# Query loads with four tokens on a partition, one key transposition moved to the DMA queue, one early matmul group moved to another step

## The chip, the core and the metric

The kernel runs on one core of one Trainium2 chip. The core has a matrix engine (TensorE, in the profile PE for its matmuls and PEld for its weight loads), a vector engine (VectorE, DVE), a scalar engine (ScalarE, ACT), a general engine (GpSimd, POOL), and SyncE (SP), which in this kernel only issues DMA transfers. Sixteen DMA engines move the data; all transfers but three of the last stores are issued by SP, one after the other, on one queue. The metric is the device time of one execution in microseconds (us), lower is better.

## The reference, cut to what matters

The first half is a recurrence over 768 tokens, for 4 batches and 8 heads of 64 columns. The second half multiplies its output by four weight matrices.

```
state = zeros(B, H, D, D)                      # B=4, H=8, S=768, D=64
for t in range(S):
    state = gamma[h] * state + outer(k[:, :, t], v[:, :, t])
    y[:, :, t] = scale * q[:, :, t] @ state
x = y.transpose(0, 2, 1, 3).reshape(B * S, H * D)        # 3072 x 512
a = x @ w1;  b = x @ w2                                  # 512 -> 1024
out = ((a * b) @ w3) @ w_out                             # 1024 -> 1024 -> 512
```

Inputs and output are 32-bit floats. Nothing nonlinear stands between w3 and w_out, so the kernel multiplies these two once, at its start.

## The kernel before, in words

**Steps.** The recurrence is worked in chunks of 128 tokens. There are 12 steps, numbered from 0 in the code: steps 0 and 1 (class `Pairs`) take 256 tokens of one batch each, steps 2 to 11 take one chunk of 128 tokens of two batches at a time. The change's title counts from one: its "steps 3 to 12" are 2 to 11 in the code, its "seventh step" is step 6, its "ninth step" is step 8. Below, the code's numbers are used, and kT(6) is the transposed keys of step 6.

**The work of one step.** All of it is in blocks of 64 tokens and 64 columns, four of which lie in the four quarters of the TensorE array at once; those are the "quarters" of the title. `scores(m)` multiplies transposed keys by queries (32 matmuls of 64x64, line 383), VectorE puts the causal mask on the result (line 390), `intra(m)` multiplies the masked scores by the values (32 matmuls, line 531), `kv(m)` forms the new part of the state (32 matmuls, line 551), `inter(m)` multiplies the old state by the queries and adds to the same PSUM banks as `intra` (line 599), and `outputs_back` multiplies by the decay and writes the block of x in half precision (line 614). The feed-forward part follows for the block of an earlier step: 16 groups of 4 matmuls with w1 and w2 (`ab`, line 636), and 16 matmuls with the product of w3 and w_out (`o_unit`, line 663).

**Order.** The order of every engine is written out by hand in `step(m)`; no scheduler moves anything. One pass of `step(m)` on TensorE is: `intra(m-1)`, `kv(m)`, `scores(m)`, `inter(m-1)`, 16 matmuls of `o_unit` for step m-2, 64 matmuls of `ab` for step m-1. Two lists change this. If m is in `EARLY`, `intra(m-1)` already stands in `step(m-1)`, after the second `ab` (four TensorE groups, 16 matmuls). If m is in `K_PE`, the keys of step m+1 are transposed by TensorE in `step(m)` (8 matmuls against an identity, line 357, and a copy by VectorE, line 358); otherwise a DMA transposes them from SBUF to SBUF (`k_dma`, line 363). Where `intra` is not early, `ended` puts a tiny copy on ScalarE behind it, and the first matmul of `inter` waits for that copy[...].

```
    EARLY = (6, 11, 12)
    K_PE = (3, 5)
```

**Queries.** They come in 512 KB tiles, two for every two steps. Tile n = 2g+e holds all 8 heads of one batch e for 256 tokens; a partition holds two consecutive tokens of each head, so that one contiguous piece in memory has 2 x 64 x 4 = 512 bytes. GpSimd casts the tile to half precision and sorts it by token (`q_cast`, line 290), a DMA transposes it (`q_dma`, line 340; the tiles of steps 2 and 3 are transposed by TensorE), and `queries(m, e, p, s, r)` cuts a matmul's moving operand out of it: 64 partitions x 2 runs of 32 columns. The order of the columns, even tokens ahead of odd ones, comes back in the masks `keep` and `keep_t`, in the decays `YS`, and in `outputs_back`, which sorts the tokens into their natural order while it writes (a step of 2 elements).

**The queue.** In `step(m)` SP issues, in this order: kT(m+1) if it is a DMA; the two stores of `o_unit`; one tile of queries for a later step (tile m+3, ahead of the keys and values in even steps, behind them in odd ones); keys and values of step m+2, each as two transfers of 256 KB in pieces of 256 bytes; and in even steps the two transpositions of queries. The loads land in staging buffers (`WST`, 22 of them). SP works strictly in order: a transposition waits on SP for its cast.

Of the kernel before, what the change touches and what calls it, by code (L numbers as in the profile page):

```python
# [12 lines left out]
MULT = mybir.AluOpType.mult  # L13
# [5 lines left out]
def kernel(  # L19
# [11 lines left out]
    nc = tc.nc  # L31
    B, H, S, D = q.shape
    C = 128
    L = 64
    WST = 22
    NCH = S // C
# [4 lines left out]
    TB = 256  # L41
    K_PE = 4

# [15 lines left out]
    def half(x):  # L59
        return slice(x * L, (x + 1) * L)  # L60

    def dma_in(dst, src):
        nc.sync.dma_start(dst, src)  # L63
# [5 lines left out]
    q_in, k_in, v_in = {}, {}, {}  # L69

    def load_q(n):

        g, e = divmod(n, 2)
        if g >= NSTEP // 2:
            return
        bp, cp = divmod(g, NCH // 2)
        q_in[n] = load_pairs(q, bp * 2 + e, cp)

    def load_pairs(src, b, cp):
        t = new_stage()  # L80
        dma_in(
            t[:, :].rearrange("p (h x) -> p h x", x=2 * D),
            src[b, :, cp * 2 * C : (cp + 1) * 2 * C, :].rearrange("h (p t) d -> p h (t d)", t=2),
        )
        return t
# [19 lines left out]
    def new_stage():  # L105
        return wstage.tile([128, 1024], FP, tag="wst", name="stg")
# [18 lines left out]
    for f in range(4, 8):  # L125
        w3_st.append(load_rows(moe_w3, f))
    for e in range(2):
        load_q(e)
        k_in[e] = load_pairs(k, e, 0)
        v_in[e] = load_pairs(v, e, 0)  # L130
    w1_st = [load_rows(moe_w1, d) for d in range(4)]
    w2_st = [load_rows(moe_w2, d) for d in range(4)]
    load_q(2)
    load_q(3)
    for m in range(2, 5):
        load_k(m)
# [14 lines left out]
    for s in range(2):  # L151
        nc.gpsimd.iota(ip_i[half(s), 0:2, :], pattern=[[1, 2], [0, H]], base=1, channel_multiplier=2)
    if_i = const.tile([128, 2, L], mybir.dt.int32, name="if_i")
    nc.gpsimd.iota(if_i[:, :, :], pattern=[[L, 2], [1, 2], [2, 32]], base=1, channel_multiplier=0)
    LGH = const.tile([128, H], FP, name="LGH")
    LGP = const.tile([128, 2, NP], FP, name="LGP")
    for h in range(H):
# [2 lines left out]
    YS = const.tile([128, 3, NP, L], FP, name="YS")  # L160
# [12 lines left out]
    def masks_and_decays():  # L173

        nc.gpsimd.memset(keep[:, :], 1.0)
        for s in range(2):
            r = slice(s * L, (s + 1) * L)
            nc.gpsimd.affine_select(
                out=keep[r, :], in_=keep[r, :], compare_op=mybir.AluOpType.is_ge, fill=0.0,
                base=0, pattern=[[1, 2], [2, 32]], channel_multiplier=-1,  # L180
            )

        nc.gpsimd.memset(keep_t[:, :, :], 1.0)
        for s in range(2):
            for t in range(2):
                nc.gpsimd.affine_select(
                    out=keep_t[half(s), t, :], in_=keep_t[half(s), t, :], compare_op=mybir.AluOpType.is_ge,
                    fill=0.0, base=-t, pattern=[[1, 2], [2, 64]], channel_multiplier=-2,
                )
        for h in range(H):  # L190
            for s in range(2):
                nc.gpsimd.memset(LGP[half((h + s) % 2), s, h // 2 : h // 2 + 1], math.log(gam[h]))
        for h in range(H):
            p, r = h // 2, (h % 2) * 64
            nc.gpsimd.memset(GS[r : r + 64, p : p + 1], gam[h] ** C)
# [11 lines left out]
    XT = {}  # L207
# [70 lines left out]
    q16s, k16s, v16s, qTs, kTs, AMs, psYs, Ts = {}, {}, {}, {}, {}, {}, {}, {}  # L278

    def q_cast(n, *engs):  # L280
        if n not in q_in:
            return
        q16s[n] = att.tile([128, 1024], HP, tag="q16", name="q16", bufs=2)
        pairs_cast(q16s[n], q_in.pop(n), *engs)

    def pairs_cast(dst, src, *engs):
        n = H // len(engs)
        for i, eng in enumerate(engs):
            hs = slice(i * n, i * n + n)
            (nc.scalar.copy if eng is nc.scalar else eng.tensor_copy)(  # L290
                dst[:, :].rearrange("i (t h d) -> i h t d", t=2, d=D)[:, hs, :, :],
                src[:, :].rearrange("i (h t d) -> i h t d", t=2, d=D)[:, hs, :, :],
            )

    def k_cast(m, engs):
        k16 = att.tile([128, 2, 512], HP, tag="k16", name="k16", bufs=3)
        k32 = k_in.pop(m)
        if len(engs) == 1:
            parts = [(k16[:, :, :].rearrange("p e x -> p (e x)"), k32[:, :, :].rearrange("p e x -> p (e x)"))]
        else:  # L300
            parts = [(k16[:, e, :], k32[:, e, :]) for e in range(2)]
        for eng, (dst, src) in zip(engs, parts):
            (nc.scalar.copy if eng is nc.scalar else eng.tensor_copy)(dst, src)  # L303
        k16s[m] = k16
# [57 lines left out]
    def k_dma(m):  # L362
        nc.sync.dma_start_transpose(
            new_kT(m)[:, :, :, :].rearrange("p e a j -> p (e a) j"),
            k16s[m][:, :, :].rearrange("p e x -> p (e x)"),
        )

    def queries(m, e, p, s, r):
        c = m % NCH
        i0 = c % 2 * 64 + s * 32  # L370
        return qTs[m // 2 * 2 + e][half(r), :, p, i0 : i0 + 32]

# [22 lines left out]
    class Pairs:  # L397
# [4 lines left out]

        def k_cast(self, *engs):
            self.k16 = att.tile([128, 1024], HP, tag="k16", name="k16", bufs=3)
            pairs_cast(self.k16, k_in.pop(self.e), *engs)

        def k_transposes(self, tag, on_dve, parts=1):
            self.kT = att.tile([128, 2, NP, 128], HP, tag="kT", name="kT", bufs=2)
# [9 lines left out]
            )  # L418

        def queries(self, r, p, s):  # L420
            return qTs[self.e][half(r), :, p, half(s)]

        def scores(self, t):
            am = att.tile([128, 2, NP, 128], HP, tag="am", name="am")
# [18 lines left out]
        def intra(self, t):  # L443
            if t == 0:
                self.y = [bank(f"Y{s}", [128, NP, 128], FP, "psY") for s in range(2)]
            for p in range(NP):
                for s in range(2):
                    for r in range(2):
                        c0 = p * 128 + r * 64
                        last = nc.tensor.matmul(  # L450
                            self.y[s][half(r), p, :], lhsT=self.v16[half(s), t, c0 : c0 + 64],
                            rhs=self.am[t][half(s), r, p, :], start=(t == 0 and p == 0),
                            stop=(s == 0 and t == 1 and p == NP - 1),
                        )
            return last
# [50 lines left out]
        def outputs_back(self, s):  # L506
            if self.e not in XT:
                XT[self.e] = xpool.tile([128, NP * 2, 2, L], HP, tag="xt", name="xt")
            nc.vector.tensor_tensor(
                XT[self.e][:, :, :, :].rearrange("p (a s) b x -> p a s (b x)", s=2)[:, :, s, :]  # L510
                .rearrange("p a (b i t) -> p a t b i", b=2, t=2),
                self.y[s][:, :, :].rearrange("p a (t b i) -> p a t b i", t=2, b=2),
                YS[:, 0:2, :, :].rearrange("p b a (t i) -> p a t b i", t=2), MULT,
            )


# [68 lines left out]
    def ended(mm, eng=None):  # L585

        mark = (eng.tensor_copy if eng else nc.scalar.copy)(mark_t[:, :], Z[0:1, 0:1])
        wait_for(mark, mm)
        return mark
# [17 lines left out]
    def outputs_back(m, s):  # L607
        if m not in XT:
            XT[m] = xpool.tile([128, NP * 2, 2, L], HP, tag="xt", name="xt")
        swap = s == 1 and m % NCH > 0  # L610
        for to in (half(0), half(1)) if swap else (slice(0, 128),):
            fr = half(1 - to.start // L) if swap else to
            n = fr.stop - fr.start
            nc.vector.tensor_tensor(  # L614
                XT[m][to, :, s, :].rearrange("p (a e) (i t) -> p a e t i", e=2, t=2),
                psYs[m][s][fr, :, :].rearrange("p (a e) (t i) -> p a e t i", e=2, t=2),
                YS[fr, s + swap, :, :].unsqueeze(2).broadcast_to((n, NP, 2, L))
                .rearrange("p a e (t i) -> p a e t i", t=2),
                MULT,
            )  # L620

# [219 lines left out]
    q_cast(3, nc.gpsimd)  # L841
    q_transposes(2, "X0", False)
    k_cast(2, (nc.gpsimd, nc.scalar))
    v_cast(2, (nc.gpsimd, nc.gpsimd))
    for f in range(2):
# [27 lines left out]

    EARLY = (6, 11, 12)

    K_PE = (3, 5)

    def step(m):  # L880

        kv_backs = []
        if m > 4:
            last = None if m in EARLY else ended(intra(m - 1))
            if m < NSTEP:
# [3 lines left out]
        else:  # L889
            inter(m - 1)  # L890
            if m == 4:
                kv_backs.append(kv(m, True))
            am_back = scores(m)
        outputs_back(m - 1, 0)
        outputs_back(m - 1, 1)
        if m >= NSTEP:
            return
        if m + 1 < NSTEP:
            k_cast(m + 1, (nc.gpsimd, nc.gpsimd))
            if m not in K_PE:  # L900
                k_dma(m + 1)
# [11 lines left out]
        for f in range(2):  # L913
            ffn[m - 1].ab(f)
        if m + 1 in EARLY:
            intra(m)
# [15 lines left out]
        for f in range(4, 8):  # L932
            if f == 6 and m in K_PE:
                k_transposes(m + 1, None)
# [43 lines left out]
```

## Time and profile before

| | |
|---|---|
| median of 3 runs | 183.44 us (183.2 to 184.47) |
| span of the profiled execution | 181.5 us |
| TensorE matmuls busy | 175.3 us (97%) |
| VectorE, ScalarE, GpSimd busy | 108.6, 71.9, 71.3 us |
| queue of SP, share of 16 DMA engines | 88.6% |
| q loads (12 of 512 KB), median from issue to landing | 6.4 us |
| k loads (20 of 256 KB), median from issue to landing | 5.6 us |
| transpositions by DMA | 8 of q (4.9 us to landing), 6 of k (4.6 us) |
| transpositions of k by TensorE in line 357 | 32 matmuls, 2.4 us |

How to read it: the busy time of an engine is the union of its instructions, and the span runs from the first instruction to the last. "To landing" is from SP's issue to the semaphore that tells of the last byte, so it contains the time in which the transfer stands in line behind earlier ones. The chain of work that ended last is a list of pieces in order of time, each with start, length and the instructions in it; a piece of "issue" is time in which an engine waited for nothing that the profile shows. In that chain a step is easily found: a block of 3.56 us in line 663 opens the large matmuls of each step, and a block of lines 531, 551, 383 and 599 (`intra`, `kv`, `scores`, `inter`) closes it.

### The profile page before, as it was taken

Reading aid. Unit: us, or ns where it says so; the run is one execution under the profiler, and the core shown is the slowest. Engines: PE = TensorE matmul, PEld = TensorE weight load, DVE = VectorE, ACT = ScalarE, POOL = GpSimd, SP = SyncE. Lnnn points to the kernel's source line nnn. Section 1 sums busy time; section 2 is a strip of 40 time slices with the busy share of each in tenths; the row PEclk is TensorE's granted clock in tenths of the full one; section 3 lists DMA queues with packets and bytes.
Section 4 is the critical chain, followed back from the end, with each engine's and each line's share of the span. In section 5 each row is a group of like instructions: output and inputs, shape, how many; then the busy total and the mean of one; then the engine's idle time right before and its main releaser. Section 6 shows DMA issues by size and latency. Waiting matters only on the chain.

```text
span 181.5 us, 6220 instructions
## 1 busy us (share of the span) xinstructions
PE 175.3 (97%) x2634; PEld 125.4 (69%) x2634; DVE 108.6 (60%) x204; ACT 71.9 (40%) x156; POOL 71.3 (39%) x127
## 2 busy tenths in 40 slices
PE   7889999999999999999999999999999999999992
PEld 2445656688766785876967858768688587685871
DVE  1246658751769669558477584494674956745430
ACT  3354845555631341524334424244243332442431
POOL 3127536964537752725427273055460350000000
PEclk9999999999999999999999999999999999999999
DMA  5999999999999999999999999999999940201203
GB/s 204 376 417 401 298 291 350 409 371 242 194 256 226 182 301 211 203 312 198 245 202 198 295 169 244 190 208 265 236 114 261 178 149 4 116 0 42 78 0 116
DMA packets 79531, 39.71 MB, mean 219 GB/s; under 512 B 57361, under 2 KB 74001, under 8 KB 79505
## 3 DMA queue, kind: packets, MB, share of 16 engines
q1 hardware_dynamic: 79072, 38.81, 88.6%
q8 instruction: 20, 0.33, 0.8%
q10 hardware_dynamic: 432, 0.52, 0.8%
q14 instruction: 7, 0.05, 0.1%
HBM read 29.36 MB, written 6.29 MB: 196 GB/s over the span
## 4 chain that ended last, share of the span: by engine, by line
PE 88%; DMA 5%; ACT 2%; SPq 1%; DVE 1%; issue 0%; ACTq 0%
PE psF L636 41%; PE psO L663 23%; DMA stg<-in_moe_w_out_dram 5%; PE psF L795 4%; PE psW L269 3%; PE psW L255 3%; PE psY L531 2%; PE psY L599 2%; PE psA L383 2%; PE psG L636 2%; PE psK L551 2%; PE psTq L328 1%; PE psW L244 1%; SPq L63 1%; PE psTk L357 1%; PE psY L450 1%
## 5 line engine op out<-in xcount | busy, mean ns | idle before, releaser
L636 PE MATMUL psF<-xt,w 128*128 128x256 f16 x672 | 76.7, 273 | 0.0
L636 PEld LDWEIGHTS <-w 128*128 128x128 f16 x704 | 68.4, 98 | 10.3
L651 DVE TENSOR_TENSOR ht<-pa,psF 128x256 f16<-128x256 f32 x88 | 36.9, 420 | 37.6 <-PE psF L636 32.0
L645 ACT COPY pa<-psF 128x256 f32<-128x256 f32 x80 | 29.8, 373 | 37.5 <-PE psF L636 37.5
L663 PE MATMUL psO<-w3o,ht 128*128 128x512 f16 (+2 forms) x200 | 43.9, 371 | 0.0
L667 ACT ACTIVATE osb<-psO 128x512 f32<-128x512 f32 (+2 forms) x25 | 14.5, 581 | 44.0 <-PE psO L663 44.0
L663 PEld LDWEIGHTS <-ht 128*128 128x128 f16 x200 | 18.5, 98 | 19.4
L614 DVE TENSOR_TENSOR xt<-psY,YS 64x512 f16<-64x512 f32 (+1 forms) x29 | 21.1, 727 | 4.8 <-PE psY L599 4.4
L310 POOL TENSOR_TENSOR v<-stg,VS 128x512 f16<-128x512 f32 x20 | 20.6, 1042 | 5.4 <-DMA stg<-in_v_dram 5.4
L303 POOL CAST k<-stg 128x512 f16<-128x512 f32 x18 | 11.0, 612 | 26.1 <-DMA stg<-in_k_dram 25.9
L290 POOL CAST q<-stg 128x1024 f16<-128x1024 f32 (+1 forms) x12 | 12.0, 1003 | 17.9 <-DMA stg<-in_q_dram 13.8
L390 DVE TENSOR_TENSOR am<-psA,keep 128x512 f16<-128x512 f32 x20 | 12.8, 682 | 0.6 <-PE psA L383 0.6
L566 POOL TENSOR_TENSOR t<-s,GS 128x512 f16<-128x512 f32 x8 | 8.3, 1039 | 7.8 <-DVE s L565 7.8
L248 DVE COPY w3t<-psW 128x1024 f16<-128x1024 f16 x8 | 5.5, 690 | 5.3 <-PE psW L244 5.3
L269 PE MATMUL psW<-wo,w3t 128*128 128x512 f16 x32 | 8.6, 381 | 0.0
L255 PE MATMUL psW<-wo,w3t 128*128 128x512 f16 x32 | 8.0, 387 | 0.7 <-ACT wo L224 0.5
L795 PE MATMUL psF<-xt,w 128*128 128x256 f16 x64 | 8.3, 273 | 0.2
L686 PE MATMUL psZ<-zeros 128*128 128x512 f16 (+1 forms) x18 | 6.6, 504 | 1.3 <-DVE zeros L143 1.3
L795 PEld LDWEIGHTS <-w 128*128 128x128 f16 x64 | 5.8, 98 | 1.8 <-ACT w L769 0.6
L573 DVE TENSOR_TENSOR t<-psK,t 128x512 f16<-128x512 f32 x9 | 6.2, 690 | 0.6 <-PE psK L551 0.5
L244 PEld LDWEIGHTS <-w3h 128*128 128x128 f16 x64 | 4.4, 103 | 3.1 <-DVE w3h L231 1.7
L225 POOL CAST wo<-stg 128x512 f16<-128x512 f32 x4 | 2.5, 613 | 10.2 <-DMA stg<-in_moe_w_out_dram 10.2
(92 smaller groups left out, 149.3 us busy)
## 6 DMA issues: line engine op xcount, KB each, us to landing
stg<-in_moe_w_dram SPq DMA_DIRECT2D x16, 512.0 KB, 8.8
stg<-in_q_dram SPq DMA_DIRECT2D x12, 512.0 KB, 6.4
out_dram<-osb SPq DMA_DIRECT2D x22, 256.0 KB, 3.3
stg<-in_k_dram SPq DMA_DIRECT2D x20, 256.0 KB, 5.6
stg<-in_v_dram SPq DMA_DIRECT2D x20, 256.0 KB, 5.6
stg<-in_moe_w_out_dram SPq DMA_DIRECT2D x4, 512.0 KB, 7.9
stg<-in_k_dram SPq DMA_DIRECT2D x2, 512.0 KB, 9.5
stg<-in_v_dram SPq DMA_DIRECT2D x2, 512.0 KB, 8.6
```

Source lines behind the costliest of these rows:

```text
L255: nc.tensor.matmul(acc[f], lhsT=w3t[f][:, g * 128 : (g + 1) * 128], rhs=WO[i][:, r, :], start=(g == 0), stop=(g == 7),)
L269: nc.tensor.matmul(self.ps[:, :], lhsT=self.t[:, g * 128 : (g + 1) * 128], rhs=WO[g // 2][:, g % 2, :], start=(g == 0), stop=(g == 7),)
L290: (nc.scalar.copy if eng is nc.scalar else eng.tensor_copy)(dst[:, :].rearrange("i (t h d) -> i h t d", t=2, d=D)[:, hs, :, :], src[:, :]. ...
L310: eng.tensor_tensor(v16[:, e, :].rearrange("j (h d) -> j h d", d=D), v32[:, e, :].rearrange("j (h d) -> j h d", d=D), VS[:, 2, :].unsqueez ...
L390: nc.vector.tensor_tensor(am[:, r, :, :], ps[r][:, :, :], keep[:, :].unsqueeze(1).broadcast_to((128, NP * 2, L)), MULT,)
L614: nc.vector.tensor_tensor(XT[m][to, :, s, :].rearrange("p (a e) (i t) -> p a e t i", e=2, t=2), psYs[m][s][fr, :, :].rearrange("p (a e) (t ...
L636: nc.tensor.matmul(ps[:, :], lhsT=W[d][:, f * 128 : (f + 1) * 128], rhs=self.x(d), start=(d == 0), stop=(d == 3),)
L645: nc.scalar.copy(self.pa[f][:, :], ps[:, :])
L651: nc.vector.tensor_tensor(self.HT[:, f, :], self.pa.pop(f)[:, :], ps[:, :], MULT)
L663: nc.tensor.matmul(psO[:, :], lhsT=self.HT[:, f, e * 128 : (e + 1) * 128], rhs=W3O[f][:, cs], start=(f == 0), stop=(f == 7),)
L667: nc.scalar.activation(osb[:, cs], psO[:, :], AF.Copy, scale=final_scale)
L795: nc.tensor.matmul(ps[f // 2][:, f % 2, :], lhsT=W[d][:, f * 128 : (f + 1) * 128], rhs=f0.x(d), start=(d == 0 and f % 2 == 0), stop=(d == ...
```

## The change

It has three parts.

1. Queries of steps 2 to 11. A tile now holds four heads of both batches: batch e lies on partitions 64e to 64e+63, and a partition holds four consecutive tokens of each head. One contiguous piece has 4 x 64 x 4 = 1024 bytes. A tile is loaded in two transfers, one for each half of the partitions, where it was one transfer before. Steps 0 and 1 keep their two tokens on a partition, but since masks and decays are shared, their queries are now read with a step of two columns. The moving operand of the other steps is 4 runs of 16 columns. The column order is now "token modulo 4", so the patterns of `if_i`, `keep`, `keep_t` and `outputs_back` follow (a step of 4 elements in the written x).
2. `K_PE` loses 5: the keys of step 6 are transposed by DMA.
3. `EARLY` has 8 in place of 11: `intra(7)` moves from the head of step 8 into step 7, and `intra(10)` from step 10 to the head of step 11.

The purpose: larger pieces make the query loads lighter for the DMA engines, and the room is used to take one transposition off TensorE.

```diff
     def load_q(n):
...
-        q_in[n] = load_pairs(q, bp * 2 + e, cp)
+        q_in[n] = new_stage()
+        for e in range(2):
+            dma_in(
+                q_in[n][half(e), :].rearrange("p (h x) -> p h x", h=4),
+                q[bp * 2 + e, hh * 4 : hh * 4 + 4, cp * 2 * C : (cp + 1) * 2 * C, :]
+                .rearrange("h (p t) d -> p h (t d)", t=4),
+            )
...
-                base=0, pattern=[[1, 2], [2, 32]], channel_multiplier=-1,
+                base=0, pattern=[[1, 4], [4, 16]], channel_multiplier=-1,
...
     def queries(m, e, p, s, r):
-        c = m % NCH
-        i0 = c % 2 * 64 + s * 32
-        return qTs[m // 2 * 2 + e][half(r), :, p, i0 : i0 + 32]
+        qT = qTs[m // 2 * 2 + p // 2][half(r), :, :, :].rearrange("p t a i -> p (t a) i")
+        i0 = e * 64 + m % NCH % 2 * 32 + s * 16
+        return qT[:, p % 2 : 8 : 2, i0 : i0 + 16]
...
         def queries(self, r, p, s):
-            return qTs[self.e][half(r), :, p, half(s)]
+            return qTs[self.e][half(r), :, p, half(s)].rearrange("d t (i u) -> d u t i", u=2)
...
-                XT[m][to, :, s, :].rearrange("p (a e) (i t) -> p a e t i", e=2, t=2),
+                XT[m][to, :, s, :].rearrange("p (a e) (i t) -> p a e t i", e=2, t=4),
...
-    EARLY = (6, 11, 12)
-
-    K_PE = (3, 5)
+    EARLY = (6, 8, 12)
+
+    K_PE = (3,)
```

Counted from the built programs: TensorE loses 8 matmuls and 8 weight loads (line 357) and its 64 instructions each of `intra(7)` and `intra(10)` stand elsewhere; VectorE loses one copy (line 358); SP issues 10 more query loads (20 halves for 10 whole tiles) and one more transposition, which stands right behind the two query transpositions that step 4 issued.

More of the change, by code (lines that the diff above doesn't have):

```diff
@@ L71, in load_q @@
     def load_q(n):
-        g, e = divmod(n, 2)
+        g, hh = divmod(n, 2)
         if g >= NSTEP // 2:
@@ L127 @@
     for e in range(2):
-        load_q(e)
+        q_in[e] = load_pairs(q, e, 0)
         k_in[e] = load_pairs(k, e, 0)
@@ L153 @@
     if_i = const.tile([128, 2, L], mybir.dt.int32, name="if_i")
-    nc.gpsimd.iota(if_i[:, :, :], pattern=[[L, 2], [1, 2], [2, 32]], base=1, channel_multiplier=0)
+    nc.gpsimd.iota(if_i[:, :, :], pattern=[[L, 2], [1, 4], [4, 16]], base=1, channel_multiplier=0)
     LGH = const.tile([128, H], FP, name="LGH")
@@ L187, in masks_and_decays @@
                     out=keep_t[half(s), t, :], in_=keep_t[half(s), t, :], compare_op=mybir.AluOpType.is_ge,
-                    fill=0.0, base=-t, pattern=[[1, 2], [2, 64]], channel_multiplier=-2,
+                    fill=0.0, base=-t, pattern=[[1, 4], [4, 32]], channel_multiplier=-2,
                 )
@@ L283, in q_cast, with token_cast @@
         q16s[n] = att.tile([128, 1024], HP, tag="q16", name="q16", bufs=2)
-        pairs_cast(q16s[n], q_in.pop(n), *engs)
-    def pairs_cast(dst, src, *engs):
-        n = H // len(engs)
+        token_cast(q16s[n], q_in.pop(n), 2 if n < 2 else 4, *engs)
+    def token_cast(dst, src, t, *engs):
+        n = 1024 // D // t // len(engs)
         for i, eng in enumerate(engs):
@@ L290, in pairs_cast @@
             (nc.scalar.copy if eng is nc.scalar else eng.tensor_copy)(
-                dst[:, :].rearrange("i (t h d) -> i h t d", t=2, d=D)[:, hs, :, :],
-                src[:, :].rearrange("i (h t d) -> i h t d", t=2, d=D)[:, hs, :, :],
+                dst[:, :].rearrange("i (t h d) -> i h t d", t=t, d=D)[:, hs, :, :],
+                src[:, :].rearrange("i (h t d) -> i h t d", t=t, d=D)[:, hs, :, :],
             )
@@ L404, in k_cast @@
             self.k16 = att.tile([128, 1024], HP, tag="k16", name="k16", bufs=3)
-            pairs_cast(self.k16, k_in.pop(self.e), *engs)
+            token_cast(self.k16, k_in.pop(self.e), 2, *engs)
         def k_transposes(self, tag, on_dve, parts=1):
@@ L510, in outputs_back @@
                 XT[self.e][:, :, :, :].rearrange("p (a s) b x -> p a s (b x)", s=2)[:, :, s, :]
-                .rearrange("p a (b i t) -> p a t b i", b=2, t=2),
-                self.y[s][:, :, :].rearrange("p a (t b i) -> p a t b i", t=2, b=2),
-                YS[:, 0:2, :, :].rearrange("p b a (t i) -> p a t b i", t=2), MULT,
+                .rearrange("p a (b i t) -> p a t b i", b=2, t=4),
+                self.y[s][:, :, :].rearrange("p a (t b i) -> p a t b i", t=4, b=2),
+                YS[:, 0:2, :, :].rearrange("p b a (t i) -> p a t b i", t=4), MULT,
             )
@@ L614, in outputs_back @@
             nc.vector.tensor_tensor(
-                XT[m][to, :, s, :].rearrange("p (a e) (i t) -> p a e t i", e=2, t=2),
-                psYs[m][s][fr, :, :].rearrange("p (a e) (t i) -> p a e t i", e=2, t=2),
+                XT[m][to, :, s, :].rearrange("p (a e) (i t) -> p a e t i", e=2, t=4),
+                psYs[m][s][fr, :, :].rearrange("p (a e) (t i) -> p a e t i", e=2, t=4),
                 YS[fr, s + swap, :, :].unsqueeze(2).broadcast_to((n, NP, 2, L))
-                .rearrange("p a e (t i) -> p a e t i", t=2),
+                .rearrange("p a e (t i) -> p a e t i", t=4),
                 MULT,
```

## The prediction

> **What bounds the kernel now.** I read the page's busy times first, then the chain of work that ended last, then the same steps by stretches, and last SP's timeline with the landings of the transpositions.
>
> ```profile
> PE 175.3 (97%) x2634; PEld 125.4 (69%) x2634; DVE 108.6 (60%) x204; ACT 71.9 (40%) x156; POOL 71.3 (39%) x127
> ...
> DMA  5999999999999999999999999999999940201203
> ```
>
> TensorE is busy 175.3 of 181.5 us, and most of the missing 6.2 us lie before the first data and behind the last matmul. So no change of waits in the middle can bring more than a fraction of a microsecond; only less work on TensorE can. The second line says that the DMA engines are full until slice 31 (about 141 us): a resource that is not the bound, but would be if it got some per cent more to do.
>
> The chain of waits, steps 5 to 8 (start, length, instructions):
>
> ```profile
> 84.41 1.75 PE psF L636 x16
> 86.16 0.38 PE psY L531 x32
> 86.54 3.60 PE psF L636 x32
> 90.14 0.45 PE psTk L357 x8
> 90.58 1.75 PE psF L636 x16
> 92.33 0.37 PE psK L551 x32
> 92.70 0.29 PE psA L383 x32
> ...
> 116.27 0.32 PE psA L383 x32
> 116.58 0.12 PE psY L599 x12
> 116.71 0.10 issue
> 116.81 0.35 PE psY L599 x20
> ```
>
> Every piece is TensorE's and each begins where the one before ends. The transposition of kT(6) costs its 0.45 us in full. In step 8 `inter(7)` stops after 12 matmuls: 0.12 + 0.10 + 0.35 = 0.57 us, where 0.29 is usual (93.00 and 128.72). No semaphore is named for that gap.
>
> The stretches of steps 5, 7, 10 and 9, each from one `o_unit` to the next:
>
> ```profile
> 80.86:93.29 12.43, 12.43 (x217) 9.36 (x218) 8.08 (x15) 4.55 (x11) 4.50 (x6) 1.00 1.19 221
> 105.08:117.16 12.08, 11.98 (x210) 9.03 (x210) 6.56 (x13) 4.27 (x11) 4.20 (x5) 1.00 1.10 197
> 140.81:152.74 11.93, 11.93 (x193) 8.85 (x194) 8.03 (x15) 4.07 (x10) 4.26 (x5) 1.00 0.63 122
> 129.01:140.81 11.80, 11.80 (x210) 8.96 (x210) 8.04 (x15) 4.27 (x11) 4.44 (x6) 1.00 1.26 196
> ```
>
> The first number is the length. A plain step takes 11.80; one with an early `intra` 11.93 (that of 10 is early), because one block more breaks the run of large matmuls; the one with the gap 12.08; the one with an early `intra` and the transposition 12.43.
>
> SP's timeline around the place where kT(6) will stand, and the landing of kT(10), the last transposition that runs under a full queue:
>
> ```profile
> 82.54 4.23 SPq L340 DMA_TRANSPOSE qT<-q  x2
> 86.86 1.02 SPq L669 DMA_DIRECT2D out_dram<-osb  x2
> 87.94 1.24 SPq L63 DMA_DIRECT2D stg<-in_k_dram  x2
> ```
>
> ```profile
> L363 SPq DMA_TRANSPOSE kT<-k x1: 2586/2586/2586, 133.5 to 133.5; - x1
> ...
> DMA to landing us min/median/max: 4.5/4.5/4.5
> ```
>
> SP has no pause here, so each transfer pushes all later ones. kT(10) lands at 133.5 + 4.5 = 138.0; `scores(10)` starts at 140.20 in the chain. Slack 2.2 us. For kT(8) it is 109.5 + 3.2 = 112.7 against 116.27: 3.6 us.
>
> [...]GpSimd's casts wait for two k loads in a row (256 KB in 256-byte pieces) that let them start at 93.10 and 94.16, 1.06 us apart, and for two q loads (512 KB in 512-byte pieces) at 43.35 and 45.18, 1.83 us apart: twice the bytes in the same 1024 packets for 1.7 times the time.[...]
>
> **The change, part by part.**
>
> Part 2, the transposition. TensorE loses 8 matmuls: −0.45 us from the chain. VectorE loses a copy of 0.69 us, hidden (60% busy). The added kT(6) stands behind the two query transpositions, which land at 87.8 and 88.6. Its cast has ended long before (the last half of k(6) is cast at 84.06 for 0.61 us), so SP does not stand still for it. Its length: kT(8), in the same place behind two query transpositions, lands 1.2 us behind the second of them (111.5 to 112.7). So kT(6) lands at about 89.8 and is wanted by `scores(6)` at 92.70 − 0.45 = 92.25: 2.4 us of slack. Queued behind it on SP are two stores, which nobody waits for, and k(7), v(7) and q(8), all 1.2 us later; their readers are casts on GpSimd (25.9 us of idle before k casts, so they simply follow), and kT(7), which has 4 us of slack (lands near 100, wanted at 104.50).
>
> Part 3, the groups. Step 7 gets the early `intra`: 12.08 to 11.93, −0.15, if the gap in step 8 goes. It should, whatever its cause: the block at the head of step 8 shrinks by 64 of its 256 instructions, and `inter(7)` no longer waits for the copy on ScalarE. Step 10 loses its early `intra`: 11.93 to 11.80, −0.13; I take −0.10 because a new block of 256 could find a gap of its own. Masked scores are ready: in step 7 six VectorE instructions of about 0.7 us (2 outputs, 2 states, 2 masks) stand between 105.08 and the early `intra` at about 110.4.
>
> Part 1, the queries. On TensorE the moving operand changes from runs of 64 bytes to runs of 32 bytes[...], and in steps 0 and 1 to a step of 4 bytes[...]. Before, two runs cost `scores` 0.29 to 0.32 us, while `kv` with its unbroken operand takes 0.27 to 0.37. The weight loads of w3 (line 244) already have a step of 4 bytes, and 8 of those transpositions take the same 0.45 us as 8 unbroken ones. I take 0. VectorE writes x with a step of 8 bytes where it was 4: the 4-byte step costs 728 ns where an unbroken write of the same size costs 682, so another 50 ns on 31 instructions, hidden: x is wanted 3.56 us (`o_unit`) after `inter`, and three outputs take 2.2. GpSimd's casts keep unbroken runs of 64: 0.
>
> On the queue a load is the large unknown. A load now takes 1.83 us. Lower end: the packet cost from the two spacings is 1.06 x 16 / 1024 = 16.6 ns at 256 bytes and 28.6 at 512, a line that gives 52.6 at 1024; 512 packets on 16 engines are then 1.68 us.[...] I take 1.83, no change: half the packets pulls down[...]. Then the queue is 1.2 us later from kT(6) on, and kT(10) keeps 2.2 − 1.2 − 0.7 = 0.3 us. Just enough; at the lower end it keeps 1.8.
>
> Sum: −0.45 − 0.15 − 0.10 = −0.70; 183.44 − 0.70 = 182.74, say 182.7.
>
> **Rivals.** (a) [...]the queue becomes the bound: slower. [...]I put it at 186.4. It would show early: q(2) and q(3) are cast at 43.35 and 45.18 and transposed by TensorE at 45.71 and 47.03. For it speaks [...]the full DMA row[...]. (b) Nothing left: the shorter chain meets a late kT(10) for half a microsecond, or the gap of step 8 turns up at the head of step 11. 183.3. (c) The finer operand slows TensorE: if the small matmuls with queries ran a quarter slower, 10 `scores` and 10 `inter` of 0.3 us and 2.4 us in steps 0 and 1 give 8.4 x 0.25 = 2.1 us: 184.8; at half speed 191. The equal times above speak against it.
>
> **How the numbers follow.** Main case 0.52, (a) 0.28, (b) 0.14, (c) 0.06. Nothing reaches 1% faster (181.6) unless the chain hides more than it shows: 0.03. Slower by over 1% (above 185.3) is most of (a) and half of (c): 0.29. Within 1%: 0.68. The range runs from 182.1 (all gaps gone, lower end of the loads) to 186.8, where the milder half of (a) ends.
>
> **What would show it.** Right: no block of line 357 near 90; step 5 at about 11.95, step 7 at 11.9, step 10 at 11.8; no idle of TensorE in front of line 383; q loads no further apart than 1.9 us. Wrong: q casts on GpSimd 2.2 us apart or more, TensorE's weight loads in line 383 waiting for the transposed keys, steps over 12.2 us from step 7 on; or, for (c), blocks of lines 383 and 599 longer than 0.35 us with no gap ahead.

## The result and the profile after

The changed kernel takes 195.56 us (median of 6 runs, 194.06 to 197.5) against 183.57 us; the ratio is 1.063 (95% interval 1.057 to 1.069). The forecast was 182.7 us, with a range from 182.1 to 186.8. Medians here are over all runs and ratios over undisturbed ones, which is why a median can stand above what its ratio says.

The page of the changed kernel, busy times and the DMA row:

```profile
PE 178.9 (93%) x2626; PEld 123.7 (64%) x2626; DVE 125.0 (65%) x203; ACT 72.7 (38%) x156; POOL 71.5 (37%) x127
...
DMA  6999999999999979999999999989999940200202
```

TensorE has 8 matmuls fewer and yet stands idle for 13.7 us of its 192.6 instead of 6.2 of 181.5. One other number has moved: VectorE has gone from 108.6 to 125.0 us with one instruction less. The groups by form say where (count, busy us, mean ns), first before and then after the change:

```profile
L614 DVE TENSOR_TENSOR xt<-psY,YS 64x512 f16<-64x512 f32 x18 | 13.1, 726 | 0.2
L614 DVE TENSOR_TENSOR xt<-psY,YS 128x512 f16<-128x512 f32 x11 | 8.0, 728 | 4.5 <-PE psY L599 4.4
```

```profile
L620 DVE TENSOR_TENSOR xt<-psY,YS 64x512 f16<-64x512 f32 x18 | 23.2, 1291 | 0.2
L620 DVE TENSOR_TENSOR xt<-psY,YS 128x512 f16<-128x512 f32 x11 | 14.1, 1296 | 5.5 <-PE psY L605 5.5
```

These are the instructions that write x (`outputs_back`, line 614 before, line 620 after): 1291 to 1296 ns where they took 726 to 728. Steps 0 and 1 have four more of the kind, which went from 728 to 1307 ns. The chain of waits through step 10, which before held TensorE pieces alone:

```profile
149.22 0.36 PE psY L605 x32
149.58 1.29 DVE xt L620
150.88 0.01 issue
150.89 1.30 DVE xt L620
152.19 0.01 issue
152.20 1.29 DVE xt L620
153.49 0.03 issue
153.52 0.70 DVE t L579
154.22 0.02 issue
154.24 0.70 DVE s L571
154.95 0.05 issue
154.99 1.49 PE psF L642 x12
```

From the end of `inter` to 154.95 VectorE sets the pace: three writes of x, then two updates of the state (lines 579 and 571). TensorE's own timeline beside it shows what it does meanwhile: 16 matmuls of `o_unit`, 3.63 us, and then a pause in front of the first product of x.

```profile
149.45 3.63 PE L669 MATMUL psO<-w3o,ht 128*128 128x512 f16 x16
153.54 7.93 PE L642 MATMUL psF<-xt,w 128*128 128x256 f16 x64 [0.47 <-DVE xt L620]
```

The 64 products take 7.93 us where 7.15 was usual before the change. Inside them TensorE pauses twice more, for the two updates of the state. In the code `kv` keeps two of the four PSUM banks that the products also draw on, and the updates, which give them back, stand behind the writes of x on VectorE. The list of waits shows the weight loads of the products waiting for each of them three times (us in all, times, longest):

```profile
PEld L642 <- DVE s L571: 1.2, 3, 0.4
PEld L642 <- DVE t L579: 1.2, 3, 0.4
```

So in steps 8 to 10 a step of about 11.8 us becomes one of 13.1 to 13.2; steps 5 and 6 take 12.67 and 12.50. The stretches of steps 7, 9 and 10, from one `o_unit` to the next (first the length, then the busy time of TensorE, its weight loads, VectorE, ScalarE and GpSimd):

```profile
109.53:122.99 13.46, 12.11 (x213) 8.85 (x209) 7.46 (x14) 4.06 (x10) 5.31 (x6) 1.00 1.25 192
136.22:149.45 13.23, 12.48 (x218) 8.70 (x209) 9.65 (x15) 4.37 (x11) 5.31 (x6) 1.00 1.27 201
149.45:162.59 13.14, 12.40 (x200) 8.61 (x193) 9.66 (x15) 4.37 (x11) 4.27 (x5) 1.00 0.64 123
```

Step 7 is the longest, and it is not VectorE's: it has 7.46 us of VectorE work, 2 us less than the two others. There TensorE waits for keys, as its timeline at the end of the step says:

```profile
122.35 0.45 PE L389 MATMUL psA<-qT,kT 64*64 64x64 f16 x32 [1.35 <-DMA kT<-k]
```

So there are two signs: a longer write of x in nearly every step, and transposed keys that come late in one. The query tiles of steps 2 and 3, the first that the change touches, are cast at 44.99 and 47.09, 2.1 us apart where it was 1.83; the experiments will show that this spacing varies too much from run to run to be a measure. How much each of the two is worth cannot be read off one profile, because a step that VectorE has stretched may give the queue more time to catch up.

### The profile page after: what moved, and what is told of

Same layout as the page of the kernel before. It is cut to its first block, busy times and chain, and to the rows that moved or that the text cites. A ratio compares the mean times of both kernels' runs of the same rounds, so it can differ in the third digit from the quotient of the medians.

```text
span 192.6 us, 6220 instructions
## 1 busy us (share of the span) xinstructions
PE 178.9 (93%) x2626; PEld 123.7 (64%) x2626; DVE 125.0 (65%) x203; ACT 72.7 (38%) x156; POOL 71.5 (37%) x127
## 4 chain that ended last, share of the span: by engine, by line
PE 37%; DMA 26%; DVE 15%; SPq 13%; issue 4%; POOL 3%; ACT 1%; ACTq 0%; POOLq 0%; DVEq 0%
PE psF L642 27%; SPq L63 12%; DVE xt L620 11%; DMA stg<-in_q_dram 6%; DMA stg<-in_k_dram 5%; PE psO L669 5%; DMA stg<-in_v_dram 4%; DMA stg<-in_moe_w_out_dram 4%; DMA stg<-in_moe_w_dram 4%; DMA kT<-k 3%; DVE s L571 1%; DVE t L579 1%; PE psY L537 1%; PE psA L389 1%; POOL k L309 1%
## 5 line engine op out<-in xcount | busy, mean ns | idle before, releaser
L642 PE MATMUL psF<-xt,w 128*128 128x256 f16 x672 | 78.3, 273 | 4.8 <-DVE xt L620 3.3
L642 PEld LDWEIGHTS <-w 128*128 128x128 f16 x704 | 67.3, 98 | 19.6 <-DVE xt L620 4.8
L657 DVE TENSOR_TENSOR ht<-pa,psF 128x256 f16<-128x256 f32 x88 | 36.3, 420 | 31.8 <-PE psF L642 31.1
L620 DVE TENSOR_TENSOR xt<-psY,YS 64x512 f16<-64x512 f32 (+1 forms) x29 | 37.3, 1293 | 5.7 <-PE psY L605 5.5
L801 PE MATMUL psF<-xt,w 128*128 128x256 f16 x64 | 8.3, 273 | 0.5 <-DVE xt L515 0.3
L801 PEld LDWEIGHTS <-w 128*128 128x128 f16 x64 | 5.8, 98 | 2.3 <-ACT w L775 0.8
```

The costliest lines, as they stand in the source:

```text
L620: nc.vector.tensor_tensor(XT[m][to, :, s, :].rearrange("p (a e) (i t) -> p a e t i", e=2, t=4), psYs[m][s][fr, :, :].rearrange("p (a e) (t ...
L642: nc.tensor.matmul(ps[:, :], lhsT=W[d][:, f * 128 : (f + 1) * 128], rhs=self.x(d), start=(d == 0), stop=(d == 3),)
L657: nc.vector.tensor_tensor(self.HT[:, f, :], self.pa.pop(f)[:, :], ps[:, :], MULT)
L801: nc.tensor.matmul(ps[f // 2][:, f % 2, :], lhsT=W[d][:, f * 128 : (f + 1) * 128], rhs=f0.x(d), start=(d == 0 and f % 2 == 0), stop=(d == ...
```

## The experiments

Theory W: the write of x with a step of 8 bytes makes VectorE the bound. Theory Q (first named as a rival to W; it is the forecast's case (a)): the query loads on partition halves set the time. All ratios are to the kernel before, measured on the same chip.

**The lists alone.** The kernel before with the two lists of the change.

```diff
-    EARLY = (6, 11, 12)
-    K_PE = (3, 5)
+    EARLY = (6, 8, 12)
+    K_PE = (3,)
```

> The kernel before with parts 2 and 3 of the change alone: EARLY = (6, 8, 12), K_PE = (3,), queries as before. Both theories (the write of x as the cause, or the query loads) leave these parts out of the loss: my own working gives -0.70 us, 182.9 against 183.6. If the transposition on the queue is what costs, it is 184 or more, with TensorE waiting in front of scores(6) or scores(10).

Ratio 0.9993 (0.9966 to 1.002): no change that can be told from none. The interval ends at −0.6 us, so the forecast of −0.70 lies just outside it. Inside the profile the forecast is there step by step. The stretches of steps 5, 7 and 10:

```profile
81.33:93.31 11.98, 11.98 (x217) 8.89 (x209) 7.44 (x14) 4.47 (x11) 4.31 (x5) 1.00 1.28 197
105.11:117.09 11.98, 11.98 (x212) 8.90 (x209) 6.55 (x13) 4.06 (x10) 5.31 (x6) 1.00 1.27 201
140.69:152.42 11.73, 11.73 (x201) 8.87 (x193) 8.03 (x15) 4.26 (x11) 4.31 (x5) 1.00 0.79 155
```

12.43, 12.08 and 11.93 became 11.98, 11.98 and 11.73: −0.75 us, against −0.70 forecast, with no wait for kT(6). The profiled span is only 0.3 us shorter, because in that execution the first `o_unit` began 0.5 us later (47.85 against 47.32).

A second part of the gain is lost where the profile does not look. The device time is longer than the span from the first to the last instruction, by 1.69 to 1.76 us in all 27 runs of the kernel before that stand beside this one, and by 2.03 to 2.15 us in all 22 runs of this one. It is so throughout: every kernel here with the old lists has 1.66 to 1.77 us outside the span, every one with the new lists, the changed kernel too, has 2.02 to 2.15, and so has the last run below, with `K_PE` empty. What in the lists does this is open; it takes nearly 0.4 us of what they save. So parts 2 and 3 shorten the steps as forecast, little of that reaches the device time, and they are no part of the loss of 12 us.

**The write step alone.** The kernel before with the changed kernel's pattern in `outputs_back`.

```diff
-                XT[m][to, :, s, :].rearrange("p (a e) (i t) -> p a e t i", e=2, t=2),
-                psYs[m][s][fr, :, :].rearrange("p (a e) (t i) -> p a e t i", e=2, t=2),
+                XT[m][to, :, s, :].rearrange("p (a e) (i t) -> p a e t i", e=2, t=4),
+                psYs[m][s][fr, :, :].rearrange("p (a e) (t i) -> p a e t i", e=2, t=4),
...
```

> The kernel before with outputs_back alone using the changed kernel's pattern (write step of 8 bytes, runs of 16). The rows of the output then stand in another order within each 64 tokens; all work is the same. Theory W: the 33 instructions take 1.29 us, each full step has 3 x 1.29 + 2 x 0.70 us on VectorE between inter and the first product with w2, and the steps grow from 11.8 to about 13.2: 192 to 195 us in all. Theory Q: at most 184, the longer writes are hidden behind o_unit.

Ratio 1.052 (1.047 to 1.058), 193.3 us. The instructions take 1288 and 1299 ns, and steps 5, 8 and 9 are about as long as in the changed kernel, step 5 longer by the 0.45 us of kT(6); the second line is step 7:

```profile
83.86:96.99 13.13, 12.67 (x226) 9.43 (x217) 9.60 (x15) 4.59 (x11) 5.02 (x7) 1.00 1.14 202
109.55:121.41 11.86, 11.86 (x213) 9.01 (x209) 7.40 (x14) 4.26 (x11) 4.27 (x5) 1.00 1.23 214
121.41:134.77 13.36, 12.64 (x219) 8.82 (x209) 9.62 (x15) 4.36 (x11) 6.18 (x7) 1.00 1.15 224
134.77:148.12 13.35, 12.51 (x217) 8.74 (x208) 9.63 (x15) 4.37 (x11) 4.27 (x5) 1.00 0.94 189
```

W holds: this one access pattern, with the old loads and the old lists, costs 9.6 us. Step 7, in which only two outputs are written, stays at 11.86 us: its 13.46 us in the changed kernel are not the work of the write.

**A unit write in the changed kernel.** The tokens are walked in natural order, so the step moves to the read of PSUM.

```diff
-    nc.gpsimd.iota(if_i[:, :, :], pattern=[[L, 2], [1, 4], [4, 16]], base=1, channel_multiplier=0)
+    nc.gpsimd.iota(if_i[:, :, :], pattern=[[L, 2], [1, L]], base=1, channel_multiplier=0)
...
-                XT[m][to, :, s, :].rearrange("p (a e) (i t) -> p a e t i", e=2, t=4),
-                psYs[m][s][fr, :, :].rearrange("p (a e) (t i) -> p a e t i", e=2, t=4),
+                XT[m][to, :, s, :].rearrange("p (a e) (i t) -> p a e i t", e=2, t=4),
+                psYs[m][s][fr, :, :].rearrange("p (a e) (t i) -> p a e i t", e=2, t=4),
```

> The changed kernel with outputs_back walking the tokens in their natural order: the write of x is unbroken, and the step lies in the read of PSUM (64 bytes) instead; YS is stored in natural order. Theory W (the 8-byte write step makes each of these VectorE instructions 1.29 us long, and VectorE becomes the bound of every step): they fall to about 0.7 us, TensorE no longer waits for x, and what is left is the slower query loads: 185 to 188 us. Theory Q (the half-partition query loads set the time, VectorE only fills the gaps): 194 to 196 as in the changed kernel. If a step in the read costs as much as one in the write, the instructions stay near 1.29 us and the time near 195.

The writes take 688 to 689 ns, less than the 726 to 728 of the kernel before: a step of 64 bytes in the read of PSUM costs nothing that shows, a step in the write does. But the ratio is still 1.035 (1.028 to 1.041), 190.7 us, above the upper edge that W had set and below the range of Q. The stretches of steps 7 to 9 and TensorE's timeline at the end of step 7:

```profile
107.93:121.91 13.98, 12.11 (x213) 8.92 (x209) 6.54 (x13) 4.06 (x10) 5.21 (x6) 1.00 1.27 193
121.91:133.80 11.89, 11.89 (x217) 8.94 (x208) 7.92 (x15) 4.26 (x11) 5.35 (x6) 1.00 1.17 228
133.80:146.41 12.61, 12.05 (x209) 8.87 (x208) 7.92 (x15) 4.25 (x11) 5.33 (x6) 1.00 1.29 199
```

```profile
121.27 0.45 PE L389 MATMUL psA<-qT,kT 64*64 64x64 f16 x32 [1.87 <-DMA kT<-k]
```

With VectorE out of the way step 8 is short again; step 7 waits for its keys, and step 9 has a pause of 0.56 us in line 642 without a named releaser. So W alone is not the whole, and the late keys point to the queue as a second cause. This one profile does not price it: of its 5.4 us over the span before, 2.8 lie ahead of the first `o_unit` (50.10 against 47.32), where TensorE waits 1.7 us for weights that were issued ahead of every changed load. The pairs of runs below do.

**Halves alone.** The kernel before, each query tile loaded as two halves of the partitions, pieces still 512 bytes.

```diff
-        q_in[n] = load_pairs(q, bp * 2 + e, cp)
+        q_in[n] = new_stage()
+        for hf in range(2):
+            t0 = cp * 2 * C + hf * C
+            dma_in(
+                q_in[n][half(hf), :].rearrange("p (h x) -> p h x", x=2 * D),
+                q[bp * 2 + e, :, t0 : t0 + C, :].rearrange("h (p t) d -> p h (t d)", t=2),
+            )
```

> The kernel before with each query tile of steps 2 to 11 loaded in two transfers, one for each half of the partitions, still two tokens on a partition (pieces of 512 bytes). Theory W: [...]the slack in front of scores(10) is 2.2 us[...]: 184 to 187. Theory Q: most of the loss of 12 us is here: 192 or more.

Ratio 1.046 (1.039 to 1.052), 192.2 us: 8.4 us more for the same bytes in the same pieces. That is over twice what W allowed (at most 187 us), and in the range that Q had set. The rows of TensorE's timeline that have a wait, in order (start, length, and in brackets the idle time ahead):

```profile
45.85 0.62 PE L334 MATMUL psTq<-ident,q 128*128 128x128 f16 x8 [0.55 <-POOL q L296]
48.89 0.62 PE L334 MATMUL psTq<-ident,q 128*128 128x128 f16 x8 [1.54 <-POOL q L296]
...
62.26 0.81 PE L669 MATMUL psO<-w3o,ht 128*128 128x512 f16 x3 [0.94 <-issue]
...
84.00 0.45 PE L389 MATMUL psA<-qT,kT 64*64 64x64 f16 x32 [0.58 <-DMA kT<-k]
122.12 0.45 PE L389 MATMUL psA<-qT,kT 64*64 64x64 f16 x32 [1.99 <-DMA kT<-k]
140.47 5.95 PE L642 MATMUL psF<-xt,w 128*128 128x256 f16 x53 [0.87 <-issue]
148.20 0.45 PE L389 MATMUL psA<-qT,kT 64*64 64x64 f16 x32 [1.14 <-DMA kT<-k]
```

These are 7.6 of the 8.0 us by which the span grew: 2.1 us for the query tiles of steps 2 and 3, 3.7 us for keys in three steps, and 1.8 us in two pauses that nothing in the profile explains. The query tiles of steps 2 and 3 are cast at 44.76 and 47.79: 3.0 us apart, not 1.83. The 187 us had taken for a load a price that no row of a trace had shown, and only one place where the lag meets TensorE. This run alone cannot say whether the halves cost it or the doubled number of transfers; the next one can.

**Every second partition.** The changed kernel with the two batches of a tile interleaved, so that each transfer reaches over the whole range of partitions (64 of them, every second one); sizes and pieces are the same. The matmuls then read their queries with a step of two columns.

```diff
-                q_in[n][half(e), :].rearrange("p (h x) -> p h x", h=4),
+                q_in[n][e::2, :].rearrange("p (h x) -> p h x", h=4),
...
-        i0 = e * 64 + m % NCH % 2 * 32 + s * 16
-        return qT[:, p % 2 : 8 : 2, i0 : i0 + 16]
+        i0 = (m % NCH % 2 * 32 + s * 16) * 2 + e
+        return qT[:, p % 2 : 8 : 2, i0 : i0 + 31 : 2]
```

> The changed kernel, but batch e of a query tile lies on every second partition (e, e+2, ...) instead of on one half; the two transfers have the same sizes and pieces. Theory P[...]: the two transfers of a tile now land about 0.8 us apart in place of 1.2, and no transposed keys come late; the write step stays, so about 192 to 194 us, as in the run with the write step alone. Theory S (two small transfers with few pieces are slow in themselves): 1.2 us apart as before, and 195.

Ratio 1.056 (1.050 to 1.062). No wait for transposed keys is left; the waits for x are all there, 0.45 to 0.77 us in front of the products of seven steps (us in all, times, longest):

```profile
PE psF L642 <- DVE xt L620: 3.6, 7, 0.8
```

The two transfers of a tile land 0.8 to 0.9 us apart (three pairs). The time is 194.0 us, at the upper edge of the range that P had set: the keys are in time, VectorE still binds.

**Both mended**, with the new lists, and the same with the old lists.

> The changed kernel with every second partition for a batch and with the unbroken write of x. Theories W and P together leave only the forecast gains, kT(6) off TensorE and the lists: 182 to 183.5 us, steps of 11.8 to 12.0. Theory S: the loads stay slow, 189 to 191. If the step of two columns in the moving operand of every scores and inter costs TensorE time, those blocks grow beyond 0.32 us and the total is above 185.

> As the kernel with both mended, but with EARLY = (6, 11, 12) and K_PE = (3, 5) as before the change. W and P: what the query layout alone brings once both faults are gone; by the chain of waits nothing, 183.2 to 184, so the lists make the 0.5 us between this and the run with both mended.

Both mended: ratio 0.996 (0.9935 to 0.9987), 183.15 us, the only version whose interval lies below 1, and by 0.4% only. With the old lists: 0.998 (0.996 to 1.001), no difference that can be told. The two intervals overlap, so the 0.5 us that I gave to the lists is not shown by the times. The landing of the two transfers of a tile, for the changed kernel and for this one (issue of the first and the second; time from issue to landing, the shorter one being that of the first):

```profile
L63 SPq DMA_DIRECT2D stg<-in_q_dram x2: 617/630/642, 105.3 to 106.0; - x2
...
DMA to landing us min/median/max: 4.9/5.2/5.6
```

```profile
L63 SPq DMA_DIRECT2D stg<-in_q_dram x2: 668/830/993, 101.3 to 102.0; - x2
...
DMA to landing us min/median/max: 4.2/4.3/4.4
```

Halves: 105.3 + 4.9 = 110.2 and 106.0 + 5.6 = 111.6, 1.4 us apart. Every second partition: 101.3 + 4.2 = 105.5 and 102.0 + 4.4 = 106.4, 0.9 apart. Same bytes, same pieces, same two transfers; only the partitions differ. This also settles the question of the run before: two transfers are not slow in themselves. And since this kernel and the changed kernel with the unit write differ in nothing but the partitions of these loads and the step with which TensorE reads them, their ratios, 0.996 and 1.035, price the halves: about 7 us.

The casts of the first two tiles start 1.55 us apart (44.47 and 46.02), and 1.50 and 1.56 in the two other runs with every second partition and the unit write, where the whole tiles of the old layout had 1.77 to 1.84 in three runs: there the larger pieces do bring a gain, though none that the time with the old lists shows. With halves of the larger pieces the same spacing was 2.10, 1.73 and 2.33 us in three runs.

**The old lists on the loaded queue.** The changed kernel with the unit write, halves, and the old lists.

> The changed kernel with the unbroken write, its query loads on partition halves, and the old lists (kT(6) by TensorE). Against the 190.7 us of the same kernel with the new lists: if a full queue makes the added transposition cost its own 1.2 us or more, this is 188 to 189.5; if the transposition hides, it is 190.7 to 191.5, since TensorE has 0.45 us more to do.

Ratio 1.028 (1.021 to 1.035), 189.5 us, against 190.7 us with the new lists; the two intervals overlap. TensorE has 0.45 us more to do here and the kernel is not slower for it. By the medians the new lists cost about 1.3 us on a queue that is late, but that is not told from nothing, and the two lists changed together, so the transposition alone is not priced. Beside the run with both mended and the old lists (0.998) this one differs by the halves alone: 1.028, about 5.4 us.

**How the write step scales.** One execution of the kernel before with a step of 16 bytes in `outputs_back` (t=8 where the write step alone had t=4).

> The kernel before with outputs_back alone writing with a step of 16 bytes (8 elements, runs of 8); rows of the output stand in another order within each 64 tokens. A write unbroken took 682 to 690 ns, with a step of 4 bytes 728, of 8 bytes 1292. If every further doubling of the step doubles the time, about 2.4 us an instruction and 215 us or more in all; if 8 bytes is a cliff[...], 1.29 us again and 193 us.

The instructions take 2402 to 2447 ns: from 8 to 16 bytes the time nearly doubles once more. The 244.4 us of the whole are one execution at a granted TensorE clock of 0.916, so they are not to be set beside the other times; VectorE's other instructions took as long as ever (the mask of line 390, 682 ns), so the length of the writes can be read.

```profile
L614 DVE TENSOR_TENSOR xt<-psY,YS 64x512 f16<-64x512 f32 x18 | 43.2, 2402 | 0.2
L614 DVE TENSOR_TENSOR xt<-psY,YS 128x512 f16<-128x512 f32 x11 | 26.5, 2447 | 4.9 <-PE psY L599 4.9
```

**One more transposition on the queue.** Both mended and `K_PE = ()`.

> Both faults mended, and K_PE empty: kT(4) is transposed by the queue as well, in step 3. TensorE loses another 0.45 us: 182.7 if kT(4) lands before scores(4), which stands at about 69 us; in step 3 the queue also carries the stores of steps 0 and 1, so if kT(4) comes late by more than 0.45 us, it is 183.2 or more.

Ratio 1.002 (0.998 to 1.006): no gain. `scores(4)` at 70.32 waits 1.85 us for its keys; on the queue they stand behind the two transpositions of queries and two stores. The wait is worth more than the 0.45 us that TensorE saves.

## Why the prediction was wrong

- The step that failed is the sentence on VectorE in part 1: "VectorE writes x with a step of 8 bytes where it was 4 ... so another 50 ns on 31 instructions, hidden". It went on in a straight line from two points, 682 ns unbroken and 728 at 4 bytes. The runs show 1292 at 8 and about 2410 at 16, so the 46 ns were not the slope. Measured, the term is 33 instructions (not 31) x 0.56 = 18.6 us of VectorE work, and it was not hidden either: three outputs take 3.9 us, not 2.2, against the 3.6 us of `o_unit`, and two updates of the state that free PSUM banks queue behind them. None of the four cases had VectorE as the bound. The warning was in the numbers shown: between `inter` and the first product there were 2.2 us of work against 3.6 us of cover, so a factor of 1.6 was enough to break it, and the price of the new step rested on no row of the trace.
- The second term that was mis-sized is the query load: taken as unchanged, 1.83 us. With the unit write the halves cost about 7 us with the new lists and 5.4 with the old. Rival (a) had the late queue and, at 186.4 us, about half of the size; of the places it counted only the waits in front of `scores`, not those for the first query tiles. I had taken a load in halves at the price of a whole one, though the kernel before has no load into half the partitions and its trace could show no price for one. Measured, the two transfers of a tile land 1.3 to 1.6 us apart on halves (six pairs), 0.8 to 0.9 on every second partition (five pairs, a sixth 1.2). As an estimate from these spacings, 256 KB in 1.4 us is about 190 GB/s, and in 0.9 us about 290. The pairs of the changed kernel among the six were issued 0.7 us apart; three more of its pairs, issued 1.2 to 2.6 us apart, land 0.8 to 1.2 us apart. The ratios show that the choice of partitions decides (1.035 on halves, 0.996 on every second partition, with the unit write and the new lists); why it does, no run shows. The sign that I had named for this, query casts 2.2 us apart, did not come: it was 2.1 in the changed kernel, and 1.73 in a run whose keys came late all the same.
- The two causes do not add. Ratios to the kernel before, all with the new lists: halves and the write step of 8 bytes 1.063; every second partition and the write step 1.056; halves and the unit write 1.035; every second partition and the unit write 0.996. With the write step in place the loads are worth about 1 us, which the intervals do not tell from nothing; without it they are worth about 7. The likely reason is that the queue has more time while VectorE stretches the steps, so that most of its lag does not reach TensorE. The profiles fit that (steps 5 and 6, ahead of the late keys, take 12.67 and 12.50 us with the write step, and the key wait of step 7 is 1.35 us, against 1.87 with the unit write), but no run isolates it.
- Right, inside the profile: −0.45, −0.15 and −0.10 us for the transposition and the lists (−0.45, −0.10, −0.20 in the run with the lists alone), and kT(6) without a wait on the old queue. The time outside the span, which the sum put at nothing, took back nearly 0.4 us. Right too: TensorE's indifference to finer operands. The 320 matmuls of `scores` are busy 4.8 us in the kernel before and in the changed one (195 ns each), and 4.7 in the last run (194 ns), the mended kernel with `K_PE` empty, whose operand has a step of two columns. That rules out case (c). The mended kernel is 0.7 us faster than before (ratio 0.996), the number of the main case, but it got there by another sum, with loads that are not those of the change: that is luck.
- Not settled: the gap inside `inter(7)` of the kernel before. With both mended and the old lists it stands in the same place, after 12 matmuls, with 0.38 us; where `intra(7)` is moved it is gone. Also without a named releaser are the pause of 0.8 to 0.9 us inside one `o_unit`, in the changed kernel and in the run with halves alone, and one in the products of step 9, of 0.56 to 1.56 us in three runs with halves.

## What to carry to other kernels

When a layout change makes an access pattern coarser, price the engine that has to undo it at the new step. If no row of the trace shows that step, take as an estimate from these runs that a doubled step may nearly double the time (here 728 to 1292 and 1292 to 2402 ns, 1.77 and 1.86 times), and ask how much cover the instruction has. Walk the loop so that the step falls on the read and the write stays unbroken; here the read was of PSUM, and 1292 ns became 688 to 689. When a load is cut into parts, let each part reach over the whole range of partitions, as every second one does: pieces of 1024 bytes on half the partitions gave a ratio of 1.028 (unit write, old lists) to the kernel before, whose pieces of 512 bytes go to all partitions, and 0.998 on every second partition. And compare the device time with the span before a saving seen in the profile is booked.

## What the runs showed of the hardware

- VectorE's multiply of 512 elements from PSUM, written in half precision: 688 ns with an unbroken write and the read of PSUM in steps of 64 bytes, 728 with a write step of 4 bytes, 1292 with 8, 2402 to 2447 with 16. Beyond 4 bytes the time grew with the bytes spanned: (1292 − 728) / 512 = 1.10 ns more for each element's 4 bytes more, and (2402 − 1292) / 512 = 2.17 for 8 more. From the unbroken write to 4 bytes it was 40 ns in all. The length of the runs of elements is no part of it: in steps 0 and 1 runs of 32 elements at 8 bytes take 1307 ns, in the other steps of the kernel before runs of 32 at 4 bytes took 728.
- TensorE read a moving operand with a step of 4 bytes at no cost that shows: in steps 0 and 1 a matmul of `scores` takes 220 ns in the changed kernel, with the step, and 220 in the kernel before, without it; one of `inter` 220 and 222. In the last run a matmul of `scores` of the other steps, with the step, takes 194 ns, 195 in the kernel before.
- Of the two 256 KB transfers of a tile the second landed 1.3 to 1.6 us behind the first on halves of the partitions (six pairs; three more of the changed kernel, issued 1.2 to 2.6 us apart, 0.8 to 1.2 us), and 0.8 to 0.9 us on every second partition (1.2 in one of six pairs).
